# Decode attention on one core: denominators moved to the values, the last probabilities turned earlier, four heads instead of five in the fixed form

## The chip, the cores and the metric

One core of one Trainium2 chip. The metric is the time of one execution in microseconds of the device (lower is better). Each variant was run several times beside runs of the kernel before on the same chip. A "span" is the first to the last instruction of one execution; it is shorter than the time by about 1.8 us.

## The reference

The output is `x + attention(layernorm(x)) + mlp(layernorm(x))` for two sequences with one query token each.

```python
x = A_x                                   # (2, 1, 448)
xn = _layernorm(x)
q = (xn @ wq) -> 16 heads of 256          # wq 448 x 4096
k, v = last 4096 rows of the caches, 8 kv heads, each for 2 query heads
p = softmax(q k^T / 16)
o = p v                                   # then concatenated, @ wo (4096 x 448)
h = xn @ w1 + b1;  mish(h) @ w2           # w1 448 x 1792
```

All is bfloat16. K and V are 2 x 8 pairs ("heads" below, numbered 0 to 15) of 4096 x 256 elements, 2 MB each: 64 MB that are read once. With the weights, 77.7 MB go through one core.

## The kernel before

For each head, K arrives in one transfer; VectorE turns it (32 x 32 blocks) in two halves ("steps" 0 to 31), PE makes the scores, ScalarE the exponentials with their row sums, VectorE turns the probabilities back, and PE multiplies them with V two heads later. Loads are all issued by one engine in program order. Names in the profiles: `k` and `kt` are K as loaded and turned, `sc` the scores, `p` and `pT` the probabilities, `sums` and `den` the row sums and the denominators, `q` the product with V in the fixed form, `oT` the scaled attention result, and `psA` the output, to which its products with wo are added. `L376` is a line of the kernel. The parts that the change and the argument touch (cuts marked `...`):

```python
def load_v(i, cuts=(0, T)):               # cuts (0, T/2, 3T/4, T) for head 15
    ...
    for lo, hi in zip(cuts, cuts[1:]):
        nc.sync.dma_start(out=t[:, lo:hi, :], in_=vin[:, lo:hi, :])

def turn_p(s):
    pT = p_pool.tile([P, TH * Q], BF16, tag="pT", name="pT", bufs=7)
    nc.vector.transpose(out=pT[:], in_=p_t.pop(s)[:])
    ...                                    # second half of a head only, from here:
    nc.vector.tensor_scalar(out=sums[:], in0=hsel, scalar1=rs[:, 0:1], ...)
    nc.vector.scalar_tensor_tensor(out=sums[:], in0=hsel, scalar=rs[:, 1:2], in1=sums[:], ...)
    den = ps_m.tile([P, rep], FP32, tag="m", name="den")
    nc.tensor.matmul(den[:], lhsT=ones_f[:], rhs=sums[:], start=True, stop=True)
    state["rec", i] = small.tile([P, rep], FP32, tag="rec", name="rec", bufs=4)
    nc.vector.reciprocal(out=state["rec", i][:], in_=den[:])

def values(i):        # ordinary form: 16 matmuls of 512 columns, then finish(i): 4 small transposes
    ...
def values_fixed(i):  # fixed form: V is the weight, 64 matmuls of 2 columns, 64 weight loads
    ...
    scale_o(i, po)

NFIX = 5              # the last five heads take the fixed form
for i in range(NK + KA):                   # NK = 16 heads, KA = 2
    ...
        for half in range(NH):
            s = i * NH + half
            if s + 1 < NSTEP:
                turn(s + 1)
            scores(s)
            if s >= 1:
                turn_p(s - 1)
            if half == 0 and i > KA:
                close(i - KA - 1)          # finish(), and mix() = product with wo each two heads
    if i == NK:
        turn_p(NSTEP - 1)
        close(i - KA - 1)
    ...
    if i >= KA:
        if i - KA < NK - NFIX:
            values(i - KA)
        else:
            values_fixed(i - KA)
    if i >= NK:
        close(i - KA)
```

In the traces each engine's work comes in program order (at 171.29 us, for instance, VectorE takes oT ahead of a K tile). The last transfers in the queue are head 15's V (a half and two quarters) and two pieces of wo.

The softmax here doesn't subtract the row's maximum and nothing guards it: scores larger than these inputs give would overflow.

Of the kernel before, what the change touches and what calls it, by code (L numbers as in the profile page):

```python
# [12 lines left out]
FP32 = mybir.dt.float32  # L13
# [21 lines left out]
def kernel(  # L35
# [13 lines left out]
    nc = tc.nc  # L49
    P = 128  # L50
# [7 lines left out]
    rep = Hq // Hkv  # L58
# [12 lines left out]
    ND = Dh // P  # L71
# [17 lines left out]
    small = ctx.enter_context(tc.tile_pool(name="small", bufs=3))  # L89
# [22 lines left out]
    for lo, hi in ((0, SC), (SC, NS)):  # L112
# [18 lines left out]
        out=rstd[:], in_=mv[:, 1:2], func=ACT.Sqrt, bias=eps_t[:], scale=1.0  # L131
# [5 lines left out]
    for r in range(2):  # L137
        n = (NS + 1 - r) // 2
        nc.vector.tensor_scalar(
            out=xn_bf[:, r : NS : 2, :, :],  # L140
# [12 lines left out]
    for b4 in range(NB):  # L153
        rows = slice(b4 * Q, (b4 + 1) * Q)
        for j in range(NQ):
            nc.vector.tensor_copy(
                out=spread[rows, b4, j * Q : (j + 1) * Q], in_=ident[rows, rows]
# [3 lines left out]
    for j in range(1, NQ):  # L161
        nc.vector.tensor_tensor(
            out=hsel, in0=hsel, in1=ident[:, j * Q : (j + 1) * Q : HS], op=ALU.add
        )
    ones_f = consts.tile([P, P], FP32)
# [10 lines left out]
    for s in range(NS):  # L176
# [7 lines left out]
        out=odd[:],  # L184
        in_=ident[:].rearrange("p (u o) -> p o u", o=2),
# [4 lines left out]
    for par in range(2):  # L190
        for x in range(NX):
            which = (par + x) % 2
            nc.vector.tensor_scalar(
                out=xs[:, par : NS : 2, x, :],
# [61 lines left out]
    def build_q(i):  # L256
        kvh, b = heads[i]
        x, h0 = divmod(kvh * rep, HH)
        t = qdiag[i % NW]
        tv = t[:].rearrange("p (n e) c -> p n e c", e=NE)  # L260
        for j in range(NQ):
            rows = slice(j * Q, (j + 1) * Q)
            for e in range(NE):
                nc.gpsimd.tensor_copy(  # L264
                    out=tv[rows, :, e, j * Q : (j + 1) * Q : HS],
                    in_=qrep[rows, :, h0 : h0 + rep, e, x, b],
                )
# [63 lines left out]
    NSTEP = len(heads) * NH  # L331
    k_t, kt_t, v_t, p_t, pT_t, wo_t = {}, {}, {}, {}, {}, {}
    state = {}

    def load_k(i):
        kvh, b = heads[i]
        t = k_pool.tile([P, T * Dh], BF16, tag="k", name="k")
        nc.sync.dma_start(  # L338
            out=t[:], in_=A_k_cache[b, kvh, s0:Sk, :].rearrange("(p t) d -> p (t d)", p=P)
        )  # L340
        k_t[i] = t

    def load_v(i, cuts=(0, T)):
        kvh, b = heads[i]
        t = v_tile(T * Dh).rearrange("p (t d) -> p t d", t=T)
        vin = A_v_cache[b, kvh, s0:Sk, :].rearrange("(p t) d -> p t d", p=P)
        for lo, hi in zip(cuts, cuts[1:]):
            nc.sync.dma_start(out=t[:, lo:hi, :], in_=vin[:, lo:hi, :])
        v_t[i] = t

    def load_wo(kvh, parts=1):
        w = wo_pool.tile([P, rep, ND * D], BF16, tag="wo", name="wo")
        r0 = kvh * rep * Dh
        win = A_wo[r0 : r0 + rep * Dh, :].rearrange("(h p c) d -> p h (c d)", h=rep, p=P)
        for u in range(parts):
            hs = slice(u * rep // parts, (u + 1) * rep // parts)
            nc.sync.dma_start(out=w[:, hs, :], in_=win[:, hs, :])
        wo_t[kvh] = w

    def turn(s):  # L360
        kt = kt_pool.tile([P, TH * Dh], BF16, tag="kt", name="kt")
        i, half = divmod(s, NH)
        k = k_t[i] if half < NH - 1 else k_t.pop(i)
        nc.vector.transpose(  # L364
            out=kt[:].bitcast(FP32),
            in_=k[:, half * TH * Dh : (half + 1) * TH * Dh].bitcast(FP32),
        )
        kt_t[s] = kt
# [26 lines left out]
# [3 lines that stand above are left out]
        pT_t[s] = pT  # L398
        i, half = divmod(s, NH)
        if half != NH - 1:  # L400
            return
        rs = state.pop(("rs", i))
        sums = small.tile([P, rep], FP32, tag="sums", name="sums")
        nc.vector.tensor_scalar(  # L404
            out=sums[:], in0=hsel, scalar1=rs[:, 0:1], scalar2=None, op0=ALU.mult
        )
        nc.vector.scalar_tensor_tensor(  # L407
            out=sums[:], in0=hsel, scalar=rs[:, 1:2], in1=sums[:], op0=ALU.mult, op1=ALU.add
        )
        den = ps_m.tile([P, rep], FP32, tag="m", name="den")  # L410
        nc.tensor.matmul(den[:], lhsT=ones_f[:], rhs=sums[:], start=True, stop=True)  # L411
        state["rec", i] = small.tile([P, rep], FP32, tag="rec", name="rec", bufs=4)
        nc.vector.reciprocal(out=state["rec", i][:], in_=den[:])  # L413

    NP = 2
    NR = NP * rep
# [1 line left out]
    def values(i):  # L418

        po = ps_o.tile([NR, NP * Dh], FP32, tag="o", name="o")  # L420
        v = v_t.pop(i)
        for u in range(T // NP):
            half, uh = divmod(u, TH // NP)
            nc.tensor.matmul(  # L424
                po[:],
                lhsT=pT_t[i * NH + half][:, uh * NP * Q : (uh + 1) * NP * Q : HS],
                rhs=v[:, u * NP : (u + 1) * NP, :].rearrange("p t d -> p (t d)"),
                start=(u == 0),
                stop=(u == T // NP - 1),
            )  # L430
        o_sb = small.tile([NR, NP * Dh], FP32, tag="o_sb", name="o_sb", bufs=1)
        nc.scalar.copy(out=o_sb[:], in_=po[:])  # L432
        state["o", i] = o_sb

    def scale_o(i, o):
        kvh, b = heads[i]
        if b == 0:
            state["oT"] = small.tile([P, ND, rep, Bsz], BF16, tag="oT", name="oT")
        nc.vector.tensor_tensor(  # L439
            out=state["oT"][:, :, :, b],  # L440
            in0=o,
            in1=state.pop(("rec", i))[:].unsqueeze(1).to_broadcast([P, ND, rep]),
            op=ALU.mult,
        )

    def finish(i):
        ov = state.pop(("o", i))[:].rearrange("r (u m c) -> r u c m", u=NP, c=ND)
        pq = ps_q.tile([P, NP * ND * NR], FP32, tag="q", name="q")
        pqv = pq[:].rearrange("p (u c r) -> p u c r", u=NP, c=ND)
        for u in range(NP):  # L450
            for c in range(ND):
                nc.tensor.transpose(pqv[:, u, c, :], ov[:, u, c, :], ident_f[0:NR, 0:NR])  # L452
        o = small.tile([P, ND, rep], FP32, tag="osum", name="osum")
        nc.vector.tensor_copy(out=o[:], in_=pqv[:, 0, :, 0:rep])  # L454
        for u in range(1, NP):
            nc.vector.tensor_tensor(
                out=o[:], in0=o[:], in1=pqv[:, u, :, u * rep : (u + 1) * rep], op=ALU.add
            )
        scale_o(i, o[:])

    def values_fixed(i):

        pq = ps_q.tile([P, NP * ND * NR], FP32, tag="q", name="q")
        po = pq[:, 0 : ND * rep].rearrange("p (c h) -> p c h", c=ND)
        vv = v_t.pop(i).rearrange("p t (m c) -> p t c m", c=ND)
        for t in range(T):
            half, th = divmod(t, TH)
            pTv = pT_t[i * NH + half][:].rearrange("p (t c) -> p t c", t=TH)
            for c in range(ND):
                nc.tensor.matmul(  # L470
                    po[:, c, :],
                    lhsT=vv[:, t, c, :],
                    rhs=pTv[:, th, 0:Q:HS],
                    start=(t == 0 and c == 0),
                    stop=(t == T - 1),
                    skip_group_check=True,
                )
        scale_o(i, po)
# [19 lines left out]
    build_q(0)  # L498
    build_q(1)
    turn(0)  # L500
    NFIX = 5

    def close(i):
        if i < NK - NFIX:
            finish(i)
        kvh, b = heads[i]
        if b == Bsz - 1:
            mix(kvh)

    for i in range(NK + KA):  # L510
        if i + 2 < NK:
            load_k(i + 2)
        if i < NK:
            load_v(i, (0, T) if i < NK - 1 else (0, T // 2, 3 * T // 4, T))
            kvh, b = heads[i]
            if b == Bsz - 1:
                load_wo(kvh, parts=1 if i < NK - 1 else 2)
# [4 lines that stand above are left out]
                scores(s)  # L522
                if s >= 1:
                    turn_p(s - 1)
                if half == 0 and i > KA:
                    close(i - KA - 1)
            if i + 2 < NK:
                build_q(i + 2)
        if i == NK:
            turn_p(NSTEP - 1)  # L530
            close(i - KA - 1)
        if i == 0:
            dense_in()
        if i == 1:
            dense_out()
# [7 lines that stand above are left out]
# [37 lines left out]
```

## Time and profile before

| | before |
|---|---|
| median time | 191.76 us (191.71 to 192.43, 3 runs) |
| profiled run | 190.9 us, span 189.1 us |
| PE, VectorE, ScalarE busy | 77%, 60%, 17% |
| DMA | 77.86 MB, 412 GB/s over the span |
| PE instructions | 1202 matmuls, 1202 weight loads |

The profiled run is 0.86 us faster than the median. Of all 54 runs of this kernel on record, 16 took 190.53 to 191.15 us and 38 took 191.35 to 192.43; below, these are its faster and its slower group (all of them are listed in the fast state). The difference looked like noise, and the prediction took it so; it is half of the story. So is a part of the page that the prediction did not use. It lists the DMA queues (packets, MB, share of the time of the 16 DMA engines):

```profile
q1 hardware_dynamic: 7796, 77.66, 97.1%
q8 instruction: 9, 0.15, 0.3%
q14 instruction: 5, 0.04, 0.1%
```

The first row is the kernel's own transfers. The second and third are fetches of the engines' programs: nine packets of 16 KB on q8, and smaller ones. They pass through the same 16 DMA engines, and they are 0.3% of their time: easy to overlook.

### The profile page before, as it was taken

What the parts mean: (1) busy time and instruction counts of PE and PEld (TensorE: products, weight loads), DVE (VectorE), ACT (ScalarE), POOL (GpSimd) and SP (SyncE); (2) the same over time, 40 slices, a digit from 0 to 9 for tenths busy, and PEclk for the clock granted to TensorE, in tenths of its full rate; (3) what the DMA queues carried; (4) which work ended last, traced back from release to release, by engine and by line L of the source; (5) the groups of instructions that cost most, each with busy time, mean ns of one, the idle gap of its engine ahead of it and who ended that gap; (6) DMA issues with size and microseconds to landing.
All of it is one profiled execution on the core that took longest, in us unless ns stands there. A gap on an engine that the chain in (4) does not pass through costs nothing.

```text
span 189.1 us, 3026 instructions
## 1 busy us (share of the span) xinstructions
PE 145.6 (77%) x1202; PEld 71.1 (38%) x1202; DVE 113.5 (60%) x193; ACT 32.0 (17%) x81; POOL 27.6 (15%) x139
## 2 busy tenths in 40 slices
PE   0142992696997799949996899779994996598973
PEld 0142381142442435323533235233532344252572
DVE  5705506988839392857658582939376764839221
ACT  6000110112122013111212022201221121110201
POOL 8004430031130030203030023003020300000000
PEclk9999996699999789997999699978999799955855
DMA  6999999999999999999999999999999999999990
GB/s 215 419 444 414 431 438 426 437 428 430 418 423 433 437 421 431 426 437 407 448 430 428 433 419 433 430 426 418 442 437 426 414 435 433 425 430 423 415 381 27
DMA packets 7816, 77.86 MB, mean 412 GB/s; under 512 B 757, under 2 KB 2809, under 8 KB 3322
## 3 DMA queue, kind: packets, MB, share of 16 engines
q1 hardware_dynamic: 7796, 77.66, 97.1%
q8 instruction: 9, 0.15, 0.3%
q14 instruction: 5, 0.04, 0.1%
q10 hardware_dynamic: 6, 0.01, 0.0%
HBM read 77.67 MB, written 0.00 MB: 411 GB/s over the span
## 4 chain that ended last, share of the span: by engine, by line
DMA 70%; DVE 21%; PE 6%; SPq 1%; issue 1%; ACT 0%; ACTq 0%
DMA k<-in_A_k_cache_dram 70%; DVE kt L364 14%; DVE pT L397 4%; PE q L470 3%; PE sc L376 1%; PE den L411 1%; DVE sums L407 1%; PE psA L214 1%; DVE sums L404 0%; SPq L114 0%; DVE oT L439 0%; SPq L275 0%; SPq L280 0%; SPq L338 0%; DVE rec L413 0%
## 5 line engine op out<-in xcount | busy, mean ns | idle before, releaser
L364 DVE STREAM_TRANSPOSE kt<-k 128x2048 f32<-128x2048 f32 x32 | 73.3, 2292 | 37.2 <-DMA k<-in_A_k_cache_dram 37.2
L376 PE MATMUL sc<-kt,qdiag 128*128 128x512 bf16 x256 | 75.2, 445 | 9.9 <-DVE kt L364 9.7
L376 PEld LDWEIGHTS <-qdiag 128*128 128x128 bf16 x256 | 25.6, 109 | 48.9 <-issue 28.0
L264 POOL COPY qdiag<-qrep 32x8 bf16<-32x8 bf16 x128 | 23.3, 215 | 122.9 <-PE sc L376 108.3
L424 PE MATMUL o<-v,pT 128*4 128x512 bf16 x176 | 39.8, 379 | 0.0
L386 ACT ACTIVATE p<-sc 128x512 bf16<-128x512 f32 x32 | 19.1, 597 | 105.1 <-PE sc L376 103.1
L424 PEld LDWEIGHTS <-pT 128*4 128x4 bf16 x176 | 14.4, 87 | 25.7 <-issue 5.8
L397 DVE STREAM_TRANSPOSE pT<-p 128x512 bf16<-128x512 bf16 x32 | 21.5, 672 | 0.0
L411 PE MATMUL den<-sums,ones_f 128*128 128x2 f32 x32 | 5.9, 253 | 15.5 <-DVE sums L407 15.4
L411 PEld LDWEIGHTS den<-sums,ones_f 128*128 128x128 f32 x32 | 5.6, 203 | 21.8 <-DVE sums L407 18.2
L432 ACT COPY o_sb<-o 4x512 f32<-4x512 f32 x11 | 6.3, 576 | 32.3 <-PE o L424 32.3
L413 DVE RECIPROCAL rec<-den 128x2 f32<-128x2 f32 x16 | 2.7, 171 | 12.6 <-PE den L411 12.6
L470 PEld LDWEIGHTS <-v 128*128 128x128 bf16 x320 | 9.1, 101 | 1.6 <-issue 1.1
L470 PE MATMUL q<-pT,v 128*128 128x2 bf16 x320 | 9.2, 165 | 0.3 <-DVE oT L439 0.3
L235 PE MATMUL qT_ps<-xs,v 128*128 128x4 bf16 x112 | 3.3, 166 | 6.2 <-DMA v<-in_A_wq_dram 3.4
L452 PE MATMUL q<-ident_f,o_sb 4*128 4x4 f32 x44 | 7.0, 261 | 0.0
L214 PE MATMUL psA<-wo,oT 128*2 128x112 bf16 x128 | 3.8, 256 | 3.5 <-DVE oT L439 3.5
L386 ACT ACTIVATION_READ_ACCUMULATOR p<-sc 128x1 f32 x32 | 6.2, 195 | 0.0
L452 PEld LDWEIGHTS q<-ident_f,o_sb 4*128 4x128 f32 x44 | 6.0, 206 | 0.2
L235 PEld LDWEIGHTS <-v 128*128 128x128 bf16 x112 | 3.1, 104 | 6.4 <-DMA v<-in_A_wq_dram 6.4
L439 DVE TENSOR_TENSOR oT<-q,rec 128x4 bf16<-128x4 f32 x5 | 0.8, 150 | 7.3 <-PE q L470 7.3
L454 DVE COPY osum<-q 128x4 f32<-128x4 f32 x11 | 1.8, 162 | 4.3 <-PE q L452 4.3
(52 smaller groups left out, 42.6 us busy)
## 6 DMA issues: line engine op xcount, KB each, us to landing
k<-in_A_k_cache_dram SPq DMA_DIRECT2D x16, 2048.0 KB, 31.4
v<-in_A_v_cache_dram SPq DMA_DIRECT2D x15, 2048.0 KB, 34.7
v<-in_B_w_dram SPq DMA_DIRECT2D x2, 1568.0 KB, 21.0
wo<-in_A_wo_dram SPq DMA_DIRECT2D x7, 448.0 KB, 31.5
v<-in_A_wq_dram SPq DMA_DIRECT2D x1, 2048.0 KB
v<-in_A_wq_dram SPq DMA_DIRECT2D x1, 1536.0 KB, 10.9
v<-in_A_v_cache_dram SPq DMA_DIRECT2D x1, 1024.0 KB, 28.6
v<-in_A_v_cache_dram SPq DMA_DIRECT2D x2, 512.0 KB, 27.3
```

The source lines that it names most:

```text
L214: nc.tensor.matmul(part(n), lhsT=lhsT, rhs=w[:, n * DO : (n + 1) * DO], start=start, stop=stop, tile_position=(0, n * Q), skip_group_check ...
L235: nc.tensor.matmul(qT_ps[:, hh, e, :], lhsT=wq_v[s][:, hh, e, :], rhs=xs[:, s, :, :].rearrange("p x b -> p (x b)"), start=(s == 0), stop=( ...
L264: nc.gpsimd.tensor_copy(out=tv[rows, :, e, j * Q : (j + 1) * Q : HS], in_=qrep[rows, :, h0 : h0 + rep, e, x, b],)
L364: nc.vector.transpose(out=kt[:].bitcast(FP32), in_=k[:, half * TH * Dh : (half + 1) * TH * Dh].bitcast(FP32),)
L376: nc.tensor.matmul(psc[:], lhsT=qdiag[i % NW][:, n * NE + e, :], rhs=ktv[:, n, e, :, :], start=(n == 0 and e == 0), stop=(n == NB - 1 and ...
L386: nc.scalar.activation(out=p_sb[:], in_=psc[:].rearrange("p t c -> p (t c)"), func=ACT.Exp, scale=scale, accum_out=state["rs", i][:, s % N ...
L397: nc.vector.transpose(out=pT[:], in_=p_t.pop(s)[:])
L411: nc.tensor.matmul(den[:], lhsT=ones_f[:], rhs=sums[:], start=True, stop=True)
L424: nc.tensor.matmul(po[:], lhsT=pT_t[i * NH + half][:, uh * NP * Q : (uh + 1) * NP * Q : HS], rhs=v[:, u * NP : (u + 1) * NP, :].rearrange( ...
L432: nc.scalar.copy(out=o_sb[:], in_=po[:])
L452: nc.tensor.transpose(pqv[:, u, c, :], ov[:, u, c, :], ident_f[0:NR, 0:NR])
L470: nc.tensor.matmul(po[:, c, :], lhsT=vv[:, t, c, :], rhs=pTv[:, th, 0:Q:HS], start=(t == 0 and c == 0), stop=(t == T - 1), skip_group_chec ...
```

## The change

The intent is to shorten what PE does after the last K tile. Part a: the denominator product leaves `turn_p` and is issued just ahead of the head's own values, where its sums are long ready. Part b: the last probabilities (step 31) are turned right after step 31's scores, ahead of the scaling of head 13. Part c: `NFIX` is 4 instead of 5, so head 11 takes the ordinary form.

```diff
-        den = ps_m.tile(...); nc.tensor.matmul(den[:], lhsT=ones_f[:], rhs=sums[:], ...)
-        state["rec", i] = ...; nc.vector.reciprocal(out=state["rec", i][:], in_=den[:])
+        state["sums", i] = sums                         # sums now has 4 buffers
+
+    def denominator(i):                                 # called first in values / values_fixed
+        den = ps_m.tile([P, rep], FP32, tag="m", name="den")
+        nc.tensor.matmul(den[:], lhsT=ones_f[:], rhs=state.pop(("sums", i))[:], ...)
+        rec = small.tile([P, rep], FP32, tag="rec", name="rec")
+        nc.vector.reciprocal(out=rec[:], in_=den[:])
+        return rec
...
-    NFIX = 5
+    NFIX = 4
...
                     turn_p(s - 1)
+                if s == NSTEP - 1:
+                    turn_p(s)
...
         if i == NK:
-            turn_p(NSTEP - 1)
             close(i - KA - 1)
```

## The prediction

> **What bounds the kernel now.** I read the page's slices and chain first, then the chain in order of time, the windows of the last microseconds, and the timelines of PE and DVE from 136 us on.
>
> ```profile
> PEclk9999996699999789997999699978999799955855
> DMA  6999999999999999999999999999999999999990
> ```
>
> Each digit is a fortieth of the span (4.7 us). DMA is full in every slice but the first and the last; 77.86 MB pass at some 430 GB/s (426 to 431 in the five long windows that I took between 3 and 168 us). So nothing that is saved between 5 and 183 us counts by itself: the next k or v tile comes when the stream brings it. The issuing engine waits for buffers and semaphores, but there are always transfers outstanding (median 31.4 us from issue to landing of a k tile), so a change of one microsecond in when a buffer comes free does not empty the stream. What is left to win is the piece between the last bytes and the end. Windows of the end (time, PE, PEld, DVE, ACT, POOL, granted clock, DMA share, GB/s):
>
> ```profile
> 183.00:183.50 0.50, 0.34 (x13) 0.28 (x11) 0.12 (x1) 0.00 (x0) 0.00 (x0) 0.50 0.95 381
> 183.50:184.00 0.50, 0.40 (x16) 0.40 (x15) 0.05 (x1) 0.00 (x0) 0.00 (x0) 0.50 0.76 292
> ...
> 184.90:185.00 0.10, 0.10 (x10) 0.10 (x8) 0.00 (x0) 0.00 (x0) 0.00 (x0) 0.50 0.20 72
> 185.00:185.10 0.10, 0.10 (x10) 0.10 (x8) 0.00 (x0) 0.00 (x0) 0.00 (x0) 0.50 0.01 0
> ```
>
> The input stream ends at about 184.95. The chain in order of time (start, length, what) shows what PE still does then:
>
> ```profile
> 168.46 2.31 DVE kt L364
> ...
> 174.64 0.58 PE den L411 x2
> 175.22 2.39 PE sc L376 x8
> 177.61 1.65 PE q L470 x64
> ...
> 179.45 0.62 DVE pT L397
> ...
> 180.49 0.58 PE den L411 x2
> 181.07 0.47 PE psA L214 x16
> 181.55 1.81 PE q L470 x64
> 183.36 0.02 issue
> 183.38 0.18 DVE oT L439
> 183.56 0.04 issue
> 183.60 1.86 PE q L470 x64
> ...
> 185.70 0.65 PE psA L214 x16
> 186.35 0.23 ACT res L547
> ```
>
> The last k tile (head 15) lands at 168.46. From there PE is the chain: scores of steps 30 and 31, values of heads 13, 14 and 15 ("q"), two output products ("psA"), two denominators ("den"). PE's last value product ends at 185.46, 0.5 us after the last bytes of wo; then come oT (0.24 with its waits), psA 0.65, the copies, the output's issue at 186.91 and its landing: about 3.6 us that the change does not touch. **So the ceiling of any gain is about 0.5 to 0.75 us**: the last psA starts at 185.70 and can't start before wo is there (184.95, plus whatever its semaphore takes).
>
> **What the Trainium skill says.** (1) "TensorE: Matmul & The Clock Gate", Part 1, section "What's actually happening": PE's clock is either full or half, by its activity in free-running windows of about 3.4 us, so idle stretches bring it down. The trace agrees in size: 8 score matmuls take 1.91 us in the group at 161.21 and 3.57 us at 170.92, where the granted clock is 0.50. The half clock is granted from about 166 to 176 and from 181 on, after PE's gaps at 159 to 161 and 163 to 165. (2) The same page, "Architectural detail: the array is 16× 32×32, not 1× 128×128": VectorE's and ScalarE's queues are strict FIFO. That matters because the change reorders DVE; the trace fits (at 171.29 oT stands ahead of kt, in program order). (3) "DMA: Bandwidth & Descriptors", section "Anatomy of one DMA": a DMA has some 2.0 us of fixed cost, mostly the receipt. The output, 1.8 KB, is issued at 186.91 and the span ends at 189.1: 2.2 us, which agrees, and stays.
>
> **The change, part by part.**
>
> *a. Denominators with the values.* The same number of den products (16, two records each, 253 ns a record) and reciprocals (171 ns), moved some two heads later, where their sums are long finished. The middle of the kernel loses waits:
>
> ```profile
> L411 PE MATMUL den<-sums,ones_f 128*128 128x2 f32 x32 | 5.9, 253 | 15.5 <-DVE sums L407 15.4
> L413 DVE RECIPROCAL rec<-den 128x2 f32<-128x2 f32 x16 | 2.7, 171 | 12.6 <-PE den L411 12.6
> ```
>
> I expect most of these 15.4 and 12.6 us to vanish from these lines, and to come back as waits for k, or for oT ahead of psA, as DMA is full there. Worth on the clock: 0, except in the tail.
>
> *b. Head 11 in the ordinary form* (16 matmuls with 512 columns instead of 64 with 2). At full clock 3.62 us (the groups at 136.89 and 149.49) for 1.79 (the group at 157.33). It would run from 157.4 to 161.05 with its den; score group 28 starts only at 161.21, when kt is ready, and PE was idle 2.09 us before it. So it fits exactly. But the transposes of its result and three small DVE operations follow (0.64 us of PE; osum, osum, oT about 0.5 us). They stand in front of psA of heads 10/11: oT comes after sums (164.88), at about 165.4, psA takes 0.37, and the scores of step 29 start at about 165.85 instead of 165.54: **+0.3 us**. Then den of head 12 (0.5) stands ahead of its values: these end at about 171.25, and the scores of step 30 start there instead of 170.92: **+0.33** (the 0.66 us of slack before them takes the rest of 0.3 + 0.5).
>
> *c. Steps 30 and 31 back to back.* Before, step 30 ended at 174.49, PE waited for sums and made den until 175.09. After, step 31 follows at once: 174.8 + 2.5 (as long as before) = 177.3, for 177.61: **-0.3**. Its kt is ready at about 173.6 (oT of head 12 at 171.4, plus 2.3).
>
> *d. From the end of the scores to the end of the last values.* Before, 185.46 - 177.61 = 7.85: values 1.65, wait for pT and sums 1.23, den 0.58, psA 0.47, values 1.81, oT 0.24, values 1.86. After: den 13 0.5, values 1.75, oT 0.25, psA 0.5, den 14 0.5, values 1.8, den 15 0.5 (it covers the wait for oT of head 14), values 1.85 = 7.65: **-0.2**. The wait of 1.23 goes, since pT and sums of head 15 now run beside the values of head 13 (ready about 1.9 us after the scores, needed 5.3 us after). But three dens stand on PE's path where one stood, and two waits for oT remain, one of them filled.
>
> Sum: the last values end at 177.3 + 7.65 = 184.95 instead of 185.46, **-0.5 us**. The last psA would start at 185.2, only 0.25 us behind wo's last bytes, so a little of it may be lost to the stream: I take -0.45. 191.76 - 0.45 = **191.3 us**.
>
> **Rivals.**
> 1. *PE's clock.* The intermediate score groups depend on it: 1.91 or 3.57 us. Head 11 in the ordinary form keeps PE busier at 157 to 161, which may shift or shorten the half-clock stretch. If steps 29 to 31 ran at full clock, scores would end about 1.5 us earlier, limited by kt at 173.6; but then the stream bounds: 0.6 to 0.75 us gained at most, about 191.1. If step 31 ran wholly at half clock (3.57 for 2.5), the end of the scores would come 1.1 us later, and the result would be about 0.6 us slower than before, 192.3. For it: half clock is granted up to 176 and the windows are free-running. Against: the before trace has ten microseconds of half clock already, and less idleness should give less.
> 2. *Head 11 collides.* If its 16 matmuls fell in a half-clock stretch they would take 7 us, push step 28 by some 3.5 us, and eat all slack before step 30: +1.5 us or more, 193. Against: the two groups before it run at full clock, with half clock only at 145.7 to 149.
> 3. *The stream takes the end.* If wo's semaphore comes 0.5 us or more after its last bytes, the last psA can't move much and the gain is 0.2 or less: 191.6. Nothing in the before trace tells the delay, as psA never waited for it.
> 4. *DVE behind den.* rec now stands before the kt of the second half of a head. If PE is late there, kt is late, and the next k buffer is released late. But at 149.5 den can follow the scores while pT of DVE ends only at 150.87, so there is no wait; and the stream has 30 us of work in hand. 0.
>
> **Range and chances.** The gain is bounded by the stream at 0.75 us, the loss by rivals 1 and 2 at about 1 us. The runs of before differ by 0.7 us among themselves (191.71 to 192.43, and 190.9 in the profiled one), which is as large as the effect. So 191.3, with 8 in 10 between 190.5 and 192.2. Two per cent are 3.8 us, far beyond what 0.5 us of PE behind the stream can give: faster 0.01, same 0.98, slower 0.01.
>
> **What would show it.** Right: input stream still ending near 185 with the same rate; no wait of PE for sums ahead of den; steps 30 and 31 adjacent; pT and sums of head 15 beside the values of head 13; last values ending about 185.0, and the last psA starting within 0.3 us of the stream's end, perhaps with a wait for a transfer of wo. Wrong: step 29 or 30 starting over 1 us later, head 11's group longer than 4 us, step 31 over 3 us, or a DMA slice below nine in the middle.

## The result, and the profile after

The changed kernel takes **190.49 us** (190.44 to 190.62, 6 runs) for 191.76 us (190.99 to 192.43, 6 runs): ratio 0.9934, 95% interval 0.9912 to 0.9957. Ratios here are the mean time of one kernel's fast runs over that of the other's of the same rounds, so not quite the ratio of the medians quoted. The time is 0.01 us below the range that was predicted; the gain is 1.27 us, where 0.45 was predicted.

The spread is as telling as the median: 0.18 us after, 1.4 us before.

Lines of the page after (span; clock; the chain, which is the work that ended last, followed back; then groups as in the prediction):

```profile
span 188.7 us, 2944 instructions
PEclk9999995799999699988999699969998799969955
DMA 82%; DVE 11%; issue 2%; PE 2%; SPq 1%; ACT 0%; ACTq 0%
L364 DVE STREAM_TRANSPOSE kt<-k 128x2048 f32<-128x2048 f32 x32 | 73.4, 2296 | 50.6 <-DMA k<-in_A_k_cache_dram 49.6
L414 PE MATMUL den<-sums,ones_f 128*128 128x2 f32 x32 | 5.1, 229 | 0.0
```

PE's 15.4 us of waiting for sums ahead of den are gone (0.0), and the waiting has moved to K (VectorE's turns: 49.6 us, before 37.2 in the trace). The chain is DMA for 82% of the span, not 70%: the end now hangs on a transfer. The chain in order of time says on which:

```profile
158.66 25.61 DMA v<-in_A_v_cache_dram
184.27 0.05 issue
184.31 0.60 PE q L479 x16
184.91 0.02 issue
184.94 0.18 DVE oT L447
185.11 0.04 issue
185.16 0.79 PE psA L214 x15
185.94 0.23 ACT res L557
```

The last quarter of head 15's V ends at 184.27; 16 of its 64 value products follow, then oT and the last product with wo. PE's timeline (start, length, what; in brackets the wait before and what ended it):

```profile
170.85 1.90 PE L376 MATMUL sc<-kt,qdiag 128*128 128x512 bf16 x8
173.89 1.91 PE L376 MATMUL sc<-kt,qdiag 128*128 128x512 bf16 x8 [1.14 <-DVE kt L364]
...
179.44 1.87 PE L479 MATMUL q<-pT,v 128*128 128x2 bf16 x64 [0.71 <-DMA v<-in_A_v_cache_dram]
181.17 0.57 PE L414 MATMUL den<-sums,ones_f 128*128 128x2 f32 x2
181.87 1.01 PE L479 MATMUL q<-pT,v 128*128 128x2 bf16 x32
183.09 0.59 PE L479 MATMUL q<-pT,v 128*128 128x2 bf16 x16 [0.21 <-DMA v<-in_A_v_cache_dram]
184.31 0.59 PE L479 MATMUL q<-pT,v 128*128 128x2 bf16 x16 [0.63 <-DMA v<-in_A_v_cache_dram]
185.16 0.68 PE L214 MATMUL psA<-wo,oT 128*2 128x112 bf16 x16 [0.26 <-DVE oT L447]
```

Steps 30 and 31 ran at full clock (1.90 and 1.91 us, predicted about 3.5 and 2.5), so PE had its scores done at 175.8 instead of 177.3 and then waited for V three times, 1.55 us in all. Between the two profiles the gain is 189.1 - 188.7 = 0.4 us of span, just what was predicted. But the profile of before is of its faster group. What the slower group loses, and the changed kernel doesn't, is the question.

### The profile page after: what moved, and what is told of

It reads as the page before. It is cut to its first block, busy times and chain, and to the rows that moved or that the text cites. A ratio compares the mean times of both kernels' runs of the same rounds, so it can differ in the third digit from the quotient of the medians.

```text
span 188.7 us, 2944 instructions
## 1 busy us (share of the span) xinstructions
PE 144.1 (76%) x1158; PEld 71.7 (38%) x1158; DVE 113.5 (60%) x195; ACT 32.5 (17%) x82; POOL 27.1 (14%) x139
## 4 chain that ended last, share of the span: by engine, by line
DMA 82%; DVE 11%; issue 2%; PE 2%; SPq 1%; ACT 0%; ACTq 0%
DMA k<-in_A_k_cache_dram 68%; DMA v<-in_A_v_cache_dram 14%; DVE kt L364 8%; DVE pT L397 2%; PE sc L376 1%; SPq L114 0%; PE psA L214 0%; SPq L338 0%; PE q L479 0%; SPq L280 0%; DVE sums L407 0%; SPq L275 0%; DVE sums L404 0%; DVE den_sb L320 0%; ACT p L386 0%
## 5 line engine op out<-in xcount | busy, mean ns | idle before, releaser
L364 DVE STREAM_TRANSPOSE kt<-k 128x2048 f32<-128x2048 f32 x32 | 73.4, 2296 | 50.6 <-DMA k<-in_A_k_cache_dram 49.6
L376 PE MATMUL sc<-kt,qdiag 128*128 128x512 bf16 x256 | 72.7, 433 | 17.6 <-DVE kt L364 15.8
L376 PEld LDWEIGHTS <-qdiag 128*128 128x128 bf16 x256 | 24.7, 105 | 57.2 <-issue 30.0
L431 PE MATMUL o<-v,pT 128*4 128x512 bf16 x192 | 43.4, 379 | 0.0
L431 PEld LDWEIGHTS <-pT 128*4 128x4 bf16 x192 | 15.8, 87 | 21.8
L439 ACT COPY o_sb<-o 4x512 f32<-4x512 f32 x12 | 6.9, 574 | 36.8 <-PE o L431 36.8
L479 PE MATMUL q<-pT,v 128*128 128x2 bf16 x256 | 7.6, 165 | 1.7 <-DMA v<-in_A_v_cache_dram 1.6
L479 PEld LDWEIGHTS <-v 128*128 128x128 bf16 x256 | 7.3, 101 | 2.0 <-DMA v<-in_A_v_cache_dram 2.0
L414 PEld LDWEIGHTS den<-sums,ones_f 128*128 128x128 f32 x32 | 6.8, 220 | 3.3 <-issue 1.7
L214 PEld LDWEIGHTS <-oT 128*2 128x2 bf16 x128 | 1.8, 87 | 11.9 <-DVE oT L447 11.7
L414 PE MATMUL den<-sums,ones_f 128*128 128x2 f32 x32 | 5.1, 229 | 0.0
L235 PEld LDWEIGHTS <-v 128*128 128x128 bf16 x112 | 3.1, 104 | 5.0 <-issue 3.0
```

The source lines that it names most:

```text
L214: nc.tensor.matmul(part(n), lhsT=lhsT, rhs=w[:, n * DO : (n + 1) * DO], start=start, stop=stop, tile_position=(0, n * Q), skip_group_check ...
L235: nc.tensor.matmul(qT_ps[:, hh, e, :], lhsT=wq_v[s][:, hh, e, :], rhs=xs[:, s, :, :].rearrange("p x b -> p (x b)"), start=(s == 0), stop=( ...
L364: nc.vector.transpose(out=kt[:].bitcast(FP32), in_=k[:, half * TH * Dh : (half + 1) * TH * Dh].bitcast(FP32),)
L376: nc.tensor.matmul(psc[:], lhsT=qdiag[i % NW][:, n * NE + e, :], rhs=ktv[:, n, e, :, :], start=(n == 0 and e == 0), stop=(n == NB - 1 and ...
L414: nc.tensor.matmul(den[:], lhsT=ones_f[:], rhs=state.pop(("sums", i))[:], start=True, stop=True)
L431: nc.tensor.matmul(po[:], lhsT=pT_t[i * NH + half][:, uh * NP * Q : (uh + 1) * NP * Q : HS], rhs=v[:, u * NP : (u + 1) * NP, :].rearrange( ...
```

## The experiments

I began with two theories: (1) PE's path after the last K tile was the bound, and part a took it away; (2) part c kept PE's clock up. Both fell with the first four runs.

### One part at a time, and PE kept warm

**a_den**: the changed kernel without b and c.

```diff
+ part a as in the diff above
  NFIX = 5, turn_p(NSTEP - 1) in its old place
```

> Part a alone: denominators with the values, five heads fixed, last turn of p in its old place. Theory 1 (PE's path after the last k tile was the bound, and taking den and the wait for sums off it lets the stream's end take over): nearly the whole gain, 0.9 to 1.3 us below the kernel before, runs within 0.3 us of each other, values of head 15 waiting for v. Theory 2 (the fourth-head form, by keeping PE's clock up, made the gain): 0.2 us or less below before, and a spread like that of before.

Measured: 191.69 us (190.91 to 191.91) for 191.65 of before, ratio 1.0006 (0.9978 to 1.0034). No gain, against theory 1. Its trace is the key. PE's timeline at the end:

```profile
183.14 0.59 PE L479 MATMUL q<-pT,v 128*128 128x2 bf16 x16 [0.21 <-DMA v<-in_A_v_cache_dram]
184.36 0.59 PE L479 MATMUL q<-pT,v 128*128 128x2 bf16 x16 [0.63 <-DMA v<-in_A_v_cache_dram]
186.19 0.35 PE L214 MATMUL psA<-wo,oT 128*2 128x112 bf16 x8 [1.24 <-DMA wo<-in_A_wo_dram]
186.72 0.36 PE L214 MATMUL psA<-wo,oT 128*2 128x112 bf16 x8 [0.18 <-DMA wo<-in_A_wo_dram]
```

Up to head 15's last values this agrees with the changed kernel within 0.05 us. Then it waits 1.24 us for wo, where the changed kernel waits for no transfer (0.26 us for oT). So PE's path is as short as in the changed kernel, and the last transfer is late. The windows (time, PE, PEld, DVE, ACT, POOL, clock, DMA share, GB/s) show what moves:

```profile
185.50:186.00 0.50, 0.00 (x0) 0.00 (x0) 0.00 (x0) 0.00 (x0) 0.00 (x0) 0.50 0.06 22
```

A share of 0.06 is one of 16 DMA engines (1/16 = 0.0625). Fifteen have finished, one is still at work. In the changed kernel the same window has no input traffic at all. The trace of a_den has the ninth q8 program fetch at 183.8 to 183.9 us, in the midst of the last transfers; the changed kernel has it at 184.9 to 185.0, at their end. The packet records do not name the engine, but their times join up: the fetch lasts from 183.89 to 184.86, a packet of the kernel's own starts at 184.85, and from there one packet follows another without a gap until 186.30, alone from 185.1 on. So the late engine is, by all that the times show, the one that carried the fetch.

**b_turn**: part b alone, den still behind its sums.

```diff
                     turn_p(s - 1)
+                if s == NSTEP - 1:
+                    turn_p(s)
...
-            turn_p(NSTEP - 1)
```

> Part b alone: the last p turned ahead, with den still issued at once behind its sums. Theory 1: slower by 0.5 to 1 us, since PE now waits some 1.9 us for the exp, pT and sums of step 31 before the values of head 13, instead of after them. If part b carries gain by itself, it is 0.3 us or more faster.

Measured: 191.99 us (190.85 to 192.91), ratio 1.0017 (0.9983 to 1.0052): 0.3 us over before by the medians, not clear of noise. The slowdown of 0.5 to 1 us that was expected is not shown. The profile has the wait as expected: 1.89 us for sums, ahead of the values of head 13. That run (192.12 us) is late by PE's path and not by a transfer: its last psA starts at 186.83, after a wait of 0.26 us for oT, when the stream had ended at 185.25. So PE's path does count once it is longer than the stream.

**c_fix4**: part c alone.

```diff
-    NFIX = 5
+    NFIX = 4
```

> Part c alone: head 11 in the ordinary form. Theory 1: within 0.3 us of before, PE still the bound at the end. Theory 2 (clock): granted clock near 1.0 from 168 to 178 us instead of 0.5, scores of steps 30 and 31 in 1.9 us each, 0.5 to 1 us faster than before.

Measured: **190.68 us** (190.43 to 190.93), ratio 0.9957 (0.9934 to 0.998). Some 1 us of the 1.27 comes with the part that the prediction had booked as a cost. Steps 30 and 31 took 1.91 us each, as theory 2 expected, so the next run was needed to tell.

**warm_before**: the kernel before with idle-time matmuls that keep PE's clock up.

```diff
+                if s in (28, 30):
+                    busy(8 if s == 28 else 2)      # 128x512 matmuls into a free bank
                 scores(s)
+                if s == 28:
+                    busy(7)
```

> The kernel before with 17 idle-time matmuls (128x512, result unused, output right) in PE's gaps ahead of and behind step 28's scores and 2 ahead of step 30's, to keep PE's clock up. If the clock of the tail makes the time of before and its spread: granted clock near 1.0 from 168 to 178 us, 0.5 to 1 us faster than before, runs within 0.4 us of each other. If the clock doesn't matter there: same as before or up to 0.3 us slower, spread as before.

Measured: 191.77 us (191.58 to 191.96), ratio 1.0014 (0.9992 to 1.0037). The page's clock line, with the whole middle and most of the end at full clock:

```profile
PEclk9999995569999999999999999999999999996955
```

(Step 30's scores still took 3.55 us; step 31's 1.91.) PE finishes earlier than in the profile of before, its first half of the last psA starts at 185.26, and then it waits 1.21 us for wo, as a_den does. So a PE that is earlier does not help by itself, against theory 2. This run alone does not clear the clock, as its 17 matmuls also lengthen PE's program and its ninth fetch comes at 184.4, not 184.8; before_again, below, does more.

### The length of PE's program

What c_fix4 has in common with the changed kernel is a shorter PE program: head 11 in the ordinary form saves 44 matmuls and 44 weight loads (1202 to 1158 of each). The new theory (F in the expectations): PE's program is fetched in 16 KB packets through the same DMA engines, and the ninth fetch meets the end of the input stream or doesn't, by the length of the program. The Trainium skill, "Trainium Architecture — The Big Picture", section "The software stack", gives 64 bytes for an instruction; that is 256 instructions in 16 KB, an estimate from that page. The runs agree: 256, 512 and 768 added PE instructions made 10, 11 and 12 packets of 9.

Four kernels, each with pairs of a weight load and a matmul without use in PE's idle time at the very start:

```diff
     add(ident[0:Bsz, 0:Bsz], x_bf[:, :], start=True)
+    idle = ps_o.tile([Bsz, Bsz], FP32, tag="o", name="idle")
+    for _ in range(N):                              # 47, 128, 81, 81
+        nc.tensor.matmul(idle[:], lhsT=ident[:, 0:Bsz], rhs=ident[:, 0:Bsz], start=True, stop=True)
```

**after_e47** (changed kernel, N = 47):

> The changed kernel with 47 pairs of weight load and matmul (128x4 weights, 2 columns, result unused) put into PE's idle time at the very start, so that its PE program is as long as that of before and each 16 KB fetch of PE's program comes 94 instructions earlier. New theory F (the stream's end is put off by the last program fetch when it falls among the last transfers): slower by 0.5 to 1.3 us than the changed kernel, 191.0 to 191.8, with the last psA waiting for wo. Theory P (PE's path): the work at the end is unchanged, so 190.5.

Measured: **191.7 us** (191.56 to 191.85). The whole gain is gone, by 94 instructions without use at 7 to 8 us, 180 us ahead of the end.

```profile
184.42 0.59 PE L484 MATMUL q<-pT,v 128*128 128x2 bf16 x16 [0.62 <-DMA v<-in_A_v_cache_dram]
186.02 0.36 PE L214 MATMUL psA<-wo,oT 128*2 128x112 bf16 x8 [1.02 <-DMA wo<-in_A_wo_dram]
```

PE's timeline of this kernel is that of a_den: all values in time (within 0.11 us of the changed kernel, though half clock on the way made steps 30 and 31 take 5.29 us together), then 1.02 us for wo. The ninth fetch is at 183.7 to 183.8.

**after_e128** (changed kernel, N = 128, one fetch more):

> The changed kernel with 128 such pairs at the start, 256 instructions, which is one 16 KB fetch more but the later fetches at the same places of the program. Theory F1 (only the fetch among the last transfers counts): 190.5 as without. Theory F2 (each fetch puts off the stream's end wherever it falls): 0.6 to 1 us slower. Theory P: 190.5.

Measured: 191.78 us (191.62 to 191.92). So F1 fell: a fetch far from the end costs as much. **before_e81** (the kernel before, N = 81):

> The kernel before with 81 pairs at the start: 162 instructions more, so that the fetches fall at the same distance from the end of its program as in the changed kernel. Theory F1: faster than before by 0.5 to 1 us (190.6 to 191.1), spread below 0.7 us. Theory F2 or P: 191.6 as before or slower.

Measured: 191.83 us (191.7 to 191.89): no faster, and without before's faster runs. It has nine fetches ahead of the last values and a tenth at the end, so F2 has it right. **a_den_e81** (part a alone, N = 81):

> Part a alone with the same 81 pairs. Theory F1: 190.5 as the changed kernel, no wait for wo. Theory F2 or P: as part a alone, 191.7.

Measured: 191.77 us (191.68 to 192.0), again as F2 says. In these three kernels it is not wo but V that is late: the last quarter of head 15's V is used from 185.7 us, where the changed kernel has it at 184.31.

**after_busy6**, the control: 6 matmuls of 512 columns at the same place, so more PE time (8.0 to some 10.7 us, where the 47 pairs took 6.9 to some 8.2) and only 12 instructions.

```diff
+    for _ in range(6):
+        nc.tensor.matmul(idle[:], lhsT=ident[:, 0:Bsz], rhs=spread[:] as 512 columns, start=True, stop=True)
```

> Control: the changed kernel with 6 matmuls of 512 columns at the start, as long on PE as some 80 of the small pairs (1.3 to 2.6 us) but only 12 instructions. Theory F: 190.5 to 190.7 as without, as no fetch is added. If it was the early PE time that made the padded kernels slow: 191.7.

Measured: 190.58 us (190.38 to 190.71). It is the number of instructions, not PE's time at the start.

**before_m48** and **a_den_m48**: 48 of the 112 pairs of the query projection left out (a wrong result), which makes PE's program as short as the changed one.

```diff
-                for s in range(NS):                 # NS = 7
+                for s in range(4):
```

> The kernel before without 48 of the 112 pairs of the query projection (a wrong result on purpose; they run at 12 to 15 us, far from the end): PE's program is then as short as the changed one, 8 program fetches before the last values instead of 9. Theory F (program fetches on one of the DMA rings put off the stream's end): 190.5 to 191.0 with wo there in time, though PE's work at the end is untouched. Theory P (PE's path at the end): 191.7 as before.

> Part a alone, without the same 48 pairs (wrong result on purpose). Theory F: 190.5 as the changed kernel, a little (0.1 to 0.4 us) below the kernel before so shortened, as PE's path then counts. Theory P: as part a alone, 191.7.

Measured: before_m48 191.2 us (190.91 to 191.78), ratio to before 0.9995 (0.9969 to 1.002): inconclusive; its profile has wo in time, with PE's last psA at 184.99, but its runs spread over 0.9 us. The shortening hardly moved its ninth fetch (184.87, and 184.81 and 184.90 in the two profiles of before), so it is a weak test. a_den_m48 190.93 us (190.87 to 190.99), ratio to before 0.9978 (0.9952 to 1.0003): 0.76 us below part a alone by the medians of different rounds, its ninth fetch at 184.84 instead of 183.89 and no wait for wo, but 0.4 us short of the changed kernel, since its last V quarter came at 184.49 and its stream ended at about 185.3. Why its stream ends a little later, I have not found.

### Why more fetches do not add up

**after_e256** (changed kernel, N = 256, two fetches more):

> The changed kernel with 256 pairs at the start, two program fetches more. Theory F with the delays adding up on one ring: another 1.0 to 1.4 us over the kernel with 128 pairs, 192.8 to 193.2. If the delay doesn't add up (a fetch goes to any ring, or the ring catches up): 191.8 as with 128 pairs.

Measured: 191.79 us (191.64 to 192.0). The time does not add up. But the windows of after_e128 and of after_e256, in this order, differ:

```profile
185.50:186.00 0.50, 0.28 (x10) 0.29 (x11) 0.00 (x0) 0.00 (x0) 0.00 (x0) 0.50 0.07 25
```

```profile
185.50:186.00 0.50, 0.44 (x16) 0.45 (x16) 0.00 (x0) 0.00 (x0) 0.00 (x0) 0.50 0.13 50
```

One engine late, then two. So I expected a third from a third fetch.

**after_e384** (N = 384):

> The changed kernel with 384 pairs at the start: 11 program fetches before the last values. Theory R (program fetches go to the rings in turn, eight of them; the ninth, tenth and eleventh each hit a ring a second time, and such a ring ends some 1.3 us after the rest): time as with 128 and 256 pairs, 191.6 to 191.9, but three rings still moving between 185.5 and 186.0 us: a DMA share of about 0.19 and 75 GB/s, where 128 pairs have 0.07 and 25, and 256 have 0.13 and 50. If fetches go to any ring at random or the delay adds up: another share, or 192.5 and more.

Measured: 191.94 us (191.68 to 191.98, 4 runs), and the window that had been asked for:

```profile
185.50:186.00 0.50, 0.33 (x12) 0.34 (x13) 0.00 (x0) 0.00 (x0) 0.00 (x0) 0.50 0.20 75
```

Three engines at 25 GB/s each, as foreseen to the digit. Each fetch beyond the eighth makes one more engine end late by about the same amount, and the end waits for the latest, whether one or three.

**after_m136** (changed kernel without 136 early pairs, wrong result; one fetch fewer):

```diff
-                for s in range(NS):
+                for s in range(2):
...
-            dense_out()
+            dense.pop("w2")
```

> The changed kernel without 136 pairs of its early matmuls (80 of the projection and 56 of the dense output; wrong result on purpose), 272 instructions and one fetch less: 7 before the last values. Theory R: no gain, 190.4 to 190.9, since the rings that had one fetch still set the end. If each fetch counts by itself: 189.3.

Measured: 190.89 us (190.76 to 191.24), within the range expected: with seven fetches before 183 us and the eighth at 184.5, nothing more is won. Seven don't help over eight, more than eight cost 1.2 us once. That fits engines that are hit in turn, where the ninth fetch is the first to fall on one for a second time. That eight engines are hit in turn is an inference; the records do not name the engine. Two things in the traces support it. The lengths of the fetches repeat after eight: in after_e384 967, 968, 951, 879, 881, 935, 929, 921 ns, then 960, 967 and 948 (the twelfth, 1115, breaks the row). And the last piece of wo reports its end on the 16 engines in two groups: in the changed kernel seven times by 184.5 us and nine times from 185.09 to 185.44; in after_m136, with one fetch fewer, eight times by 184.4 and eight from 185.03 to 185.69.

The runs by the number of q8 fetches ahead of the last values (before 183 us; the next one follows at 183.7 to 185.3):

| fetches before 183 us | next fetch | kernels: median us |
|---|---|---|
| 7 | 184.5 (the eighth) | after_m136 190.89 |
| 8 | 183.7 to 184.5, among the last transfers | a_den 191.69, after_e47 191.7, warm_before 191.77 |
| 8 | 184.7 to 185.3, at their end | changed 190.49, c_fix4 190.68, after_busy6 190.58, ac_late 190.61, v_eighth 190.69, a_den_m48 190.93, before_m48 191.2; b_turn 191.99 (by PE's path); before: both groups |
| 9, 10, 11 | 184.8 to 185.2, at the end | 9: after_e128 191.78, before_e81 191.83, a_den_e81 191.77; 10: after_e256 191.79; 11: after_e384 191.94 |

### What a and b are worth, and a further cut

**ac_late** (a and c, without b):

```diff
-                if s == NSTEP - 1:
-                    turn_p(s)
...
+            turn_p(NSTEP - 1)
```

> Parts a and c without b: the last p is turned in its old place, behind the scaling of head 13. With a in place den of head 15 is needed only after the values of head 14, so b should be worth nothing: 190.4 to 190.7. If b matters, 0.3 us or more slower.

Measured: 190.61 us (190.52 to 190.76), ratio to before 0.9945 (0.9924 to 0.9966). Part b is worth some 0.1 us by the medians of different rounds, if anything.

**v_eighth**:

```diff
-    (0, T // 2, 3 * T // 4, T)
+    (0, T // 2, 3 * T // 4, 7 * T // 8, T)
```

> The changed kernel with the last quarter of the last v loaded in two pieces. If the stream's end is the bound: the values that wait for the very last v piece are 8 pairs instead of 16 (0.3 us instead of 0.59), so psA starts some 0.3 us sooner, unless wo is then not there: 190.2 to 190.5. If PE were the bound: unchanged.

Measured: 190.69 us (190.6 to 190.91): not better than the changed kernel, and worse than expected. psA's first half does start earlier (184.98), but its second half now waits 0.33 us for wo, until 185.66. Nothing tried here beats the changed kernel.

### A second profile of the kernel before

**before_again**: the kernel before, unchanged.

> The kernel before, unchanged, for a second profile of it. Its runs fall into two groups (190.5 to 191.1 and 191.4 to 192.1 us), and the profile on hand is of the first, with the ninth program fetch at 184.9 us, behind the last transfers. Theory R: if this profile is of the second group, the ninth fetch comes before 184.9 us, one ring (share 0.07, 25 GB/s or less) moves until about 186.3, and the last psA waits for wo; if it is of the first group, none of this.

Measured: 192.03 and 192.04 us, one of the slower group. PE's timeline at the end:

```profile
184.54 0.59 PE L470 MATMUL q<-pT,v 128*128 128x2 bf16 x16 [0.47 <-DMA v<-in_A_v_cache_dram]
185.38 0.36 PE L214 MATMUL psA<-wo,oT 128*2 128x112 bf16 x8 [0.26 <-DVE oT L439]
186.93 0.36 PE L214 MATMUL psA<-wo,oT 128*2 128x112 bf16 x8 [1.18 <-DMA wo<-in_A_wo_dram]
```

PE was *earlier* here than in the fast profile (psA at 185.38 for 185.70; half clock for 3.4 us from 171.4, where the fast profile has it for 10 us from 166.2), and the run is 1.1 us slower, by one wait of 1.18 us for wo. The expectation was right in this and wrong in how: no engine moved data until 186.3. The data ended at about 185.3; the ninth fetch came at 184.8 to 184.9, as in the fast profile; and one packet alone is left behind it (the DMA queues of the window 185.55 to 186.2 us):

```profile
DMA packets 1, 0.00 MB, mean 0 GB/s; under 512 B 1, under 2 KB 1, under 8 KB 1
```

By the packet records it has 4 bytes, which I take for the write that reports a transfer as done (each piece ends with one on each engine), and it starts at the moment the 16 KB fetch (0.96 us long) ends. The Trainium skill, "DMA: Bandwidth & Descriptors", section "Queues, rings and completion order", has the rule that fits: the semaphore increment "lands only after every earlier write from that SDMA engine, across its queues". Here it stood behind a program fetch. That accounts for the time up to 185.87; the report itself lands at 186.88, 1.01 us later, where a_den, after_e47 and warm_before have 0.37 to 0.44 us, and for that rest of 0.6 us I have no record. In the fast profile all data were done by 185.1. So I read before's two groups as a race between the ninth fetch and the end of wo. The time of the fetch alone does not tell them apart (184.81 in the fast profile, 184.90 in the slower one, 184.77 to 184.97 in c_fix4, after_busy6, ac_late and the changed kernel); what differs is whether the engine of the fetch still has something of wo behind it. That this sets the groups rests on one profile of each.

## Why the prediction was wrong, point by point

**What bounds the kernel: wrong for most runs, and the step that failed.** "The input stream ends at about 184.95" and "PE's last value product ends at 185.46" were read from one profile of 190.9 us and applied to a median of 191.76. In the slower group of before, as far as its one profile (before_again) shows, PE is done with the values by 185.2 and the end waits for wo until 186.93. The prediction saw the difference of 0.86 us and called it scatter. This is the step that failed: wo was taken to be there at 184.95 in every run, so PE's path of a faster run was shortened and the saving taken from the median of mostly slower ones, which PE's path does not bound. What the change took away there is the wait for wo of some 1.2 us (1.18 in before_again), not 0.45 us of PE. On equal footing the number comes out, 190.9 - 0.45 = 190.45 for 190.49 measured, but partly by luck: V, not PE's work, set the end (below).

**Rival 3, "the stream takes the end": right in kind, wrong in sign.** It was written as a limit to the gain, with nothing to tell wo's delay; the landing records of that trace do have it, with the last report of wo at 185.33, some 0.3 us after its last packet (185.04). That the change could move the stream's end itself was not among the rivals, as DMA was full and no transfer had changed. The change did so through PE's program: part a alone has the ninth fetch at 183.89, in the way of wo; with the 88 instructions fewer of part c it is at 184.97, and padding it back (after_e47, 183.73) brings the wait for wo back. Against the two profiles of before (184.81 and 184.90) the shift is small, so there the reading rests on the race above.

**Part a: right in mechanism, worth little alone.** The waits for sums vanished from den (15.4 to 0.0 us) and came back as waits for K, as predicted. In the tail, a_den's last values end at 184.95 instead of 185.46, the 0.5 us of the prediction, with no gain in time (191.69 for 191.65): its ninth program fetch comes at 183.9, among the last transfers, and wo is late.

**Part b (in the prediction's d): right in mechanism, worth next to nothing beyond a.** "pT and sums of head 15 now run beside the values of head 13" holds (176.56 to 177.64 beside 175.78 to 177.57); ac_late shows some 0.1 us.

**Part c (the prediction's b): the size was wrong, and the sign.** It was booked as +0.3 and +0.33 us of PE. These delays are there (step 29's scores at 165.78, predicted 165.85; head 12's values end at 170.86, predicted 171.25), but measured alone the part gains 0.97 us by the medians (191.65 to 190.68), and when the changed kernel's program is brought back to the old length without touching its work (after_e47), the gain is gone.

**The prediction's c and d, steps 30 to the end:** PE ran these at full clock (1.90 and 1.91 us), which was rival 1, and stood 1.5 us ahead of the predicted 177.3; the stream then held it, as rival 1 also said. The last values end at 184.91 (predicted 184.95) and the last psA starts at 185.16 (predicted 185.2), but by waits for V, not by the sum of PE's work. The agreement of the end is part luck.

**Clock as a cause of the spread:** I suspected it after the result. The two profiles of before speak against it, as the slower run had the fuller clock and the earlier PE; warm_before agrees, but its fetch moved too. (One reading of the prediction was off: the trace has the half clock from 179.8, not 181. Nothing rests on it.)

## What to carry to other kernels

When transfers fill a kernel to its end, look at everything that passes through the DMA engines, program fetches too: adding 94 instructions on PE at the very start cost the changed kernel 1.2 us at its end. Before you subtract from a median, check that the profile is of a typical run, and look at what the runs in the other group wait for. And try the parts of a change singly: the one that was to cost time made most of the gain, and the one that was to bring it brought nothing by itself.

## What the Trainium skill lacked or had wrong

- "Trainium Architecture — The Big Picture", section "The software stack", tells of the program being moved to the engines when it is loaded. Here it is fetched during the run: 9 packets of 16 KB on q8, 10 to 12 when PE's program was 256 to 768 instructions longer. The skill does have this on another page, "Runtime: NRT & Kernel Launch", section "Instruction fetch mechanics", with blocks of 16 KiB, as here; but it calls the cost of crossing a block "mostly hidden". Here a ninth fetch among the last transfers cost 1.2 us (191.7 for 190.5 us).
- "DMA: Bandwidth & Descriptors", section "Queues, rings and completion order", puts refills on row 14 as runtime-internal. In these traces q14 has 5 packets in the page's count, and PE's program comes on q8; whether the profile numbers its queues as that page does its rows, no run shows.
- No page found gives the cost of a fetch to the transfers beside it, or says that it can show at the end: one, two and three engines still moving 25, 50 and 75 GB/s at 185.5 to 186.0 us with nine, ten and eleven fetches before 183 us, and nothing won with seven instead of eight (190.89 us).
- The rule on semaphore increments of the same section fits the one run that bears on it: a 4-byte write at the end of a 0.96 us fetch, and 1.18 us of waiting for wo, of which some 0.6 us stay unexplained.
- "TensorE: Matmul & The Clock Gate", Part 1, section "What's actually happening", has the half clock follow an idle window of about 3.4 us. In the kernel before, gaps of 2.09 and 1.82 us with 1.9 us of work between them sufficed for it (half clock from 166 us). Its section "A second HAM failure mode: psum-queue depth-cycling" does tell of short idles that make the clock swing, but gives no length.
